# First four chunks of a retention and feed-forward kernel in another order, weight transfers to all partitions, other pacing

## The chip, the cores and the metric

The kernel runs on one core of one Trainium2 chip. The metric is the device time of one execution in microseconds (us). Five engines work side by side, each through its own queue in order: PE (matrix products, with PEld for its weight loads), DVE (the vector engine), ACT (the scalar engine), POOL (GpSimd) and SP, which here only issues transfers (DMAs).

## What is computed

```python
scores = scale * np.matmul(q, k.transpose(0, 1, 3, 2))     # 8 batches, 8 heads, 576 tokens, head width 64
ret = scores * Dmat                                        # gamma_h ** (t - s) for s <= t, else 0
attn_out = np.matmul(ret, v)
x = attn_out.transpose(0, 2, 1, 3).reshape(B * S, H * D)   # 4608 tokens x 512
h = np.maximum(x @ w_in, 0.0)                              # w_in 512 x 2048
return h * h @ w_out                                       # w_out 2048 x 512
```

`w_in` and `w_out` arrive as 64-bit floats. The kernel rounds them to 32 bits itself.

## The kernel before

**Retention in chunks.** Each batch's 576 tokens are cut in chunks of 128, 128, 128, 128 and 64 (`N_CH` = 40 in all), each of two halves of 64 tokens. For a chunk `load` brings k, q and v to tiles `k_ld`, `q_ld`, `v_ld` (one transfer each, on SP), and for the first five also a slice of the decay table `dq`. Then come

- `turn` (T below): 16 transposes of k and q on PE into `t_ps` (L363), a copy of k to `kT` on ACT (L369), and a product with `dq` to `qT` on DVE (L371);
- `scores` (S): products of `kT` and `qT` into `sc_ps` (L384), the mask on DVE into `ret` (L387), and the scaling of `v_ld` on POOL (L389). `t_ps` and `sc_ps` are one buffer, so that `turn` of the next chunk waits until DVE has read the scores;
- `retain_a` (X): the second half's own products into `x_ps` (L401), and the growth of the state in `u_ps` (L407), which ACT copies to `u_sb` (L413);
- `retain_b` (U): products of the state `u_sb` with `qT` into `x_ps` (L441);
- `retain_c` (X): the first half's own products and the second growth, and ACT's copy of the finished `x_ps` to the block of x (L462). `x_ps` is one buffer, so that the next `retain_a` waits for that copy.

**Feed-forward in blocks.** Nine blocks of 512 tokens. Block 0 is done by 16 plain steps `first_in` (each 4 products of 512 columns, L523; ACT's relu L528 and DVE's square L531 follow). Blocks 1 to 8 use a scheme with 7 products for 8 (`PRODUCTS`): 28 steps `ffn_in` each (L557), for which DVE first makes four sums of x (`sum_x`, L485 to L488), and sums of the results (L499 to L502) that SP writes to `g_dram` (L503). The second product with `w_out` (L736) runs behind all of this, from 640 us on.

**Conversion of the weights.** `w_in` comes in 16 pieces of 512 KB (`fetch_w`, before in two transfers of 64 partitions each, L184) into six raw buffers. Each piece takes five steps (`round_parts`): `one` (DVE L204, ACT L206), `two` (DVE L210, ACT L211), `three`, `four`, `five` (DVE L214, L217, L220). `convert(n)` emits the next n of these steps. A piece must be through before its `first_in`.

**What sets the order.** The program is written out by hand: per chunk `i` the main loop (L639) emits retain_a, retain_b, scores, turn and retain_c, with `convert` and `ffn` between them. `ffn` emits as many feed-forward steps as the pacing number `owed` allows, which grows with the chunk's tokens. Engines take what is emitted in that order, so that a step that waits holds all that is behind it on its engine. The steps of a block join the list `steps` when all its tokens are through.

## Time and profile before

| | us |
|---|---|
| median of 3 executions | 1045.21 (1044.27 to 1048.78) |
| the profiled execution | 1044.61 |
| its span, first to last instruction | 1042.8 |
| PE busy in it | 987.2 (95%) |
| DVE busy | 754.7 (72%) |
| ACT busy | 184.0 (18%) |
| POOL busy | 80.2 (8%) |

In the profile's rows a line reads: start or count, duration, engine, line of the kernel, operation, tile written, tiles read, shape, and in square brackets how long the engine was idle before and who ended that. One matrix product on 32-bit numbers is two records. PEclk is the granted clock of PE as a share of full speed.

### The profile page before, as it was taken

The numbers are of one execution on the slowest core, as the hardware profiler recorded it, in microseconds if no ns is written. First come the engines' busy times: TensorE is split into PE (matmuls) and PEld (weight loads), VectorE is DVE, ScalarE is ACT, GpSimd is POOL, SyncE is SP. The second block draws the span as 40 slices with busy tenths as digits, with TensorE's granted clock in tenths as the row PEclk, the third lists the DMA queues.
The fourth block names the chain that finished last, engine by engine and source line by source line (L and its number), as shares of the span: only waits on it lengthen the run. The fifth ranks groups of instructions, "written<-read, shape, count | busy, mean of one in ns | idle before, by whom it ended". The sixth has DMA issues, their size and how long they took to land.

```text
span 1042.8 us, 23785 instructions
## 1 busy us (share of the span) xinstructions
PE 987.2 (95%) x10376; PEld 868.3 (83%) x10376; DVE 754.7 (72%) x1398; ACT 184.0 (18%) x421; POOL 80.2 (8%) x82
## 2 busy tenths in 40 slices
PE   3699898999999999999999999999999999999998
PEld 2555457888887888878788788999999999999998
DVE  2567659766788888887796668677676777766775
ACT  2444322111221222222221110000000000000000
POOL 1111102001111101101011010000000000000000
PEclk9999899999999999999999999999999999999999
DMA  9998365645579778768746897853736536465351
GB/s 203 200 202 204 116 173 182 176 136 170 173 206 277 214 187 295 225 176 296 183 157 245 325 402 276 339 205 121 266 144 236 203 122 249 154 245 193 132 202 41
DMA packets 177927, 215.06 MB, mean 206 GB/s; under 512 B 116128, under 2 KB 126368, under 8 KB 168864
## 3 DMA queue, kind: packets, MB, share of 16 engines
q1 hardware_dynamic: 177824, 213.56, 65.2%
q8 instruction: 81, 1.33, 0.5%
q14 instruction: 22, 0.18, 0.1%
HBM read 125.19 MB, written 88.34 MB: 205 GB/s over the span
## 4 chain that ended last, share of the span: by engine, by line
PE 87%; DVE 7%; DMA 2%; ACT 2%; issue 1%; SPq 1%; ACTq 0%; DVEq 0%
PE o_b L736 16%; PE h_b L557 16%; PE o_c L736 10%; PE o_a L736 10%; PE h_c L557 10%; PE h_a L557 10%; PE h_ps L523 5%; PE x_ps L401 3%; PE t_ps L363 2%; PE x_ps L441 2%; PE sc_ps L384 2%; DMA a<-g_dram 1%; PE u_ps L407 1%; DVE room L564 1%; DVE ret L387 1%
## 5 line engine op out<-in xcount | busy, mean ns | idle before, releaser
L557 PE MATMUL h_b<-room,w 128*128 128x256 f32 x736 | 178.7, 386 | 7.5 <-DVE room L486 4.9
L557 PEld LDWEIGHTS h_b<-room,w 128*128 128x128 f32 x736 | 137.8, 191 | 28.5 <-issue 5.8
L736 PE MATMUL o_b<-w,room 128*128 128x128 f32 x1168 | 144.5, 275 | 1.3 <-DVE room L708 1.3
L736 PEld LDWEIGHTS o_b<-w,room 128*128 128x128 f32 x1168 | 137.2, 192 | 1.5 <-DVE room L708 1.4
L736 PE MATMUL o_c<-w,room 128*128 128x128 f32 x1008 | 123.0, 275 | 0.0
L736 PEld LDWEIGHTS o_c<-w,room 128*128 128x128 f32 x1008 | 117.7, 192 | 0.0
L557 PE MATMUL h_c<-room,w 128*128 128x256 f32 x480 | 115.6, 384 | 0.7 <-DVE room L571 0.7
L557 PE MATMUL h_a<-room,w 128*128 128x256 f32 x448 | 108.3, 385 | 0.0
L557 PEld LDWEIGHTS h_c<-room,w 128*128 128x128 f32 x480 | 89.6, 190 | 13.6 <-DVE room L571 1.1
L557 PEld LDWEIGHTS h_a<-room,w 128*128 128x128 f32 x448 | 84.2, 191 | 12.4 <-issue 0.5
L736 PE MATMUL o_a<-w,a 128*128 128x128 f32 x688 | 85.9, 275 | 1.3 <-DMA a<-g_dram 1.3
L736 PEld LDWEIGHTS o_a<-w,a 128*128 128x128 f32 x688 | 81.3, 192 | 1.5 <-issue 1.5
L564 DVE SCALAR_TENSOR_TENSOR room<-room 128x512 f32<-128x512 f32 x96 | 69.9, 728 | 3.3
L574 POOL TENSOR_TENSOR room<-room 128x512 f32<-128x512 f32 x32 | 34.4, 1075 | 460.4 <-ACT room L573 448.2
L401 PE MATMUL x_ps<-ret,v_ld 64*64 64x64 f32 x1152 | 54.9, 239 | 11.9 <-ACT room L462 9.1
L401 PEld LDWEIGHTS x_ps<-ret,v_ld 64*64 64x64 f32 x1152 | 44.7, 147 | 23.9 <-issue 20.6
L747 ACT COPY r<-o_a 128x128 f32<-128x128 f32 x54 | 14.4, 266 | 277.9 <-PE o_a L736 237.2
L523 PE MATMUL h_ps<-room,w 128*128 128x512 f32 x128 | 62.2, 631 | 0.0
L576 DVE TENSOR_TENSOR room<-h_b,room 128x512 f32<-128x512 f32 x32 | 22.1, 690 | 43.8 <-PE h_b L557 43.8
L389 POOL TENSOR_TENSOR v_ld<-v_ld,dv 128x512 f32<-128x512 f32 (+1 forms) x40 | 45.5, 1139 | 96.0 <-DMA v_ld<-in_v_dram 89.7
L387 DVE TENSOR_TENSOR ret<-sc_ps,msk 128x512 f32<-128x512 f32 (+1 forms) x40 | 27.4, 684 | 29.3 <-PE sc_ps L384 29.3
L407 PE MATMUL u_ps<-v_ld,k_ld 64*64 64x64 f32 x1024 | 47.6, 238 | 0.0
(92 smaller groups left out, 1330.0 us busy)
## 6 DMA issues: line engine op xcount, KB each, us to landing
g_dram<-room SPq DMA_DIRECT2D x36, 1792.0 KB, 7.3
a<-g_dram SPq DMA_DIRECT2D x43, 1024.0 KB, 6.1
room<-g_dram SPq DMA_DIRECT2D x20, 1024.0 KB, 6.2
w<-w_dram SPq DMA_DIRECT2D x7, 1792.0 KB, 10.9
out_dram<-room SPq DMA_DIRECT2D x18, 512.0 KB, 3.2
k_ld<-in_k_dram SPq DMA_DIRECT2D x32, 256.0 KB, 5.4
q_ld<-in_q_dram SPq DMA_DIRECT2D x32, 256.0 KB, 6.1
v_ld<-in_v_dram SPq DMA_DIRECT2D x32, 256.0 KB, 6.5
```

Source lines behind the costliest of these rows:

```text
L363: nc.tensor.transpose(p[:, h, j, hp, :], loaded[i][j][rows(h), 2 * hp:2 * hp + 2, :], ident[rows(h), rows(h)])
L384: nc.tensor.matmul(sc[rows(h), e, hp, :], lhsT=kT[rows(e), hp, t], rhs=qT[rows(e), hp, t], start=True, stop=True, skip_group_check=True)
L387: nc.vector.tensor_tensor(r[:cs], sc[:cs], msk[:cs].to_broadcast([cs, 2, HP, CH]), op=ALU.mult)
L389: nc.gpsimd.tensor_tensor(vs[:cs], vs[:cs], dv[:cs, :, ci:ci + 1].to_broadcast([cs, H, D]), op=ALU.mult)
L401: own.append(lambda g=g, e=e, b=b, head=head: nc.tensor.matmul(x_at(g, e, b, h), lhsT=s["vs"][rows(h), head, :], rhs=s["ret"][rows(h), e, ...
L407: grow.append(lambda hp=hp, e=e, head=head: nc.tensor.matmul(u_ps[0][rows(e), hp, :], lhsT=loaded[i][1][rows(1 - h), head, :], rhs=s["vs"] ...
L523: nc.tensor.matmul(p.rearrange("p h t -> p (h t)"), lhsT=w[:, c, :], rhs=xT[0][:, c, :], start=(c == 0), stop=(c == N_DM - 1))
L557: nc.tensor.matmul(p[:, mm, :], lhsT=w[:, c, :], rhs=xs[n][right][:, c, :], start=(j in OPENS and mm == 0 and c == 0), stop=(j in CLOSES a ...
L564: nc.vector.scalar_tensor_tensor(t, t, 0.0, t, op0=ALU.max, op1=ALU.mult)
L574: nc.gpsimd.tensor_tensor(g["A11"], g["A11"], g["A11"], op=ALU.mult)
L576: nc.vector.tensor_tensor(g["A22"], p, p15, op=ALU.add)
L736: nc.tensor.matmul(p, lhsT=s["lefts"][left][:, m, :], rhs=w_out[j][:, m, WO_SLOT[right], :], start=(i in OPENS and m == 0), stop=(i in CLO ...
```

## The change

- **First four chunks.** Chunks 0 to 3 (`N_EARLY`) run in a loop of their own, with no feed-forward step between: per turn of the loop retain_a, retain_b, retain_c of the chunk before, then scores and turn. Weight conversion begins at the second turn, and SP brings the first piece behind chunk 1's data instead of chunk 0's. `retain_c` of these chunks has a two-column copy on ACT ahead of its products (before, the last two chunks alone had it), so that these products wait for ACT.
- **w_in and the heads.** A piece of `w_in` is now one transfer to 128 partitions, in the weights' plain order. So that x comes out in that order, heads 4 and 5, and 6 and 7, change places in k and q while they are loaded: k and q are loaded in three transfers each (four heads, then two of two heads) instead of one, and the decay table is turned to match.
- **Pacing.** `first_in` steps run over 768 tokens instead of 1024, with four convert steps ahead of each instead of three; blocks 1 to 3 are spread over the next 1280 tokens; from there 28 steps for each 512 tokens, as before.
- **x in two parts.** In `retain_c` the state's copy now comes ahead of the copy of x; feed-forward steps that must come before x's buffer is written again are emitted between the two parts of a chunk that lies across two blocks; and a block's steps join the list right behind the copy.

```diff
         got = {}
         for name, src, pool in (("k", k, ld4), ("q", q, ld3), ("v", v, ld4)):
             t = got[name] = pool.tile([128, H, D], F32, tag=name, name=f"{name}_ld")
-            nc.sync.dma_start(t[:cs], src[b, :, c0:c0 + cs, :].rearrange("h s d -> s h d"))
+            at = src[b, :, c0:c0 + cs, :].rearrange("h s d -> s h d")
+            if name == "v":
+                nc.sync.dma_start(t[:cs], at)
+            else:
+                nc.sync.dma_start(t[:cs, 0:H // 2, :], at[:, 0:H // 2, :])
+                for e in range(2):
+                    nc.sync.dma_start(t[:cs, H // 2 + e::2, :], at[:, H // 2 + 1 - e::2, :])
             if i < NCH and name == "q":
                 nc.sync.dma_start(dq[:, :, c0:c0 + cs], decay_q[:, :, c0:c0 + cs])
         if i == 0:
...
         wi, m, e = pieces[j]
         f = (m + e * N_M) * 128
         if wi == 0:
-            return moe_w_in.rearrange("(b c d) f -> b d c f", b=2, c=N_DM)[:, :, :, f:f + 128]
+            return moe_w_in.rearrange("(c p) f -> p c f", p=128)[:, :, f:f + 128]
         return moe_w_out[f:f + 128, :].rearrange("p (c f) -> p c f", c=N_DM)
     def piece_dst(j):
...
-    def bring(t, j):
-        src = piece_src(j)
-        for b in range(2 if pieces[j][0] == 0 else 1):
-            if pieces[j][0] == 0:
-                nc.sync.dma_start(t[64 * b:64 * b + 64], src[b])
-            else:
-                nc.sync.dma_start(t, src)
     def fetch_w(j):
         if j < len(pieces) and wide:
-            bring(raw_of(j).bitcast(I64).rearrange("p (c f) -> p c f", c=N_DM), j)
+            nc.sync.dma_start(raw_of(j).bitcast(I64).rearrange("p (c f) -> p c f", c=N_DM), piece_src(j))
...
     nc.gpsimd.memset(exp_bias, -896.0 * 2.0 ** 23)
     for i in range(3):
         load(i)
-        fetch_raw(1)
+        fetch_raw(min(i, 1))
     ident = only.tile([128, 128], F32, name="ident")
     make_identity(nc, ident)
...
-    HEADS = [(g, e, b, 4 * b + 2 * g + e) for g in range(H // 4) for e in range(2) for b in range(2)]
+    HEADS = [(hp, e, e if hp < HP // 2 else 1 - e) for hp in range(HP) for e in range(2)]
...
-    def x_at(g, e, b, h):
-        return xp[0][rows(b), e, 0:256].rearrange("p (g t) -> p g t", g=2)[:, g, CH * h:CH * h + CH]
+    def x_at(hp, b, h):
+        return xp[0][rows(b), hp // 2, 0:256].rearrange("p (g t) -> p g t", g=2)[:, hp % 2, CH * h:CH * h + CH]
-        for g, e, b, head in HEADS:
-            own.append(lambda g=g, e=e, b=b, head=head: nc.tensor.matmul(
-                x_at(g, e, b, h), lhsT=s["vs"][rows(h), head, :], rhs=s["ret"][rows(h), e, 2 * b + g, :],
-                start=clears(b, e), stop=False, skip_group_check=True))
-        for hp in range(HP):
-            for e in range(2):
-                head = 2 * hp + e
-                grow.append(lambda hp=hp, e=e, head=head: nc.tensor.matmul(
-                    u_ps[0][rows(e), hp, :], lhsT=loaded[i][1][rows(1 - h), head, :], rhs=s["vs"][rows(1 - h), head, :],
-                    start=(ci == 0 and h == 1 and hp == 0), stop=(hp == HP - 1), skip_group_check=True))
+        for hp, e, b in HEADS:
+            own.append(lambda hp=hp, e=e, b=b: nc.tensor.matmul(
+                x_at(hp, b, h), lhsT=s["vs"][rows(h), 2 * hp + b, :], rhs=s["ret"][rows(h), e, hp, :],
+                start=clears(b, hp // 2), stop=False, skip_group_check=True))
+            grow.append(lambda hp=hp, e=e, b=b: nc.tensor.matmul(
+                u_ps[0][rows(e), hp, :], lhsT=loaded[i][1][rows(1 - h), 2 * hp + e, :], rhs=s["vs"][rows(1 - h), 2 * hp + b, :],
+                start=(ci == 0 and h == 1 and hp == 0), stop=(hp == HP - 1), skip_group_check=True))
...
             if 2 * ci + h == 0:
                 continue
             u = u_sb[(2 * ci + h) % 3]
-            for g in range(2):
-                for b in range(2):
-                    for e in range(2):
-                        nc.tensor.matmul(x_at(g, e, b, h), lhsT=u[rows(e), 2 * b + g, :],
-                                         rhs=s["qT"][rows(e), 2 * b + g, CH * h:CH * h + CH],
-                                         start=clears(b, e), stop=False, skip_group_check=True)
+            for hp, e, b in HEADS[0:2] + HEADS[4:6] + HEADS[2:4] + HEADS[6:8]:
+                nc.tensor.matmul(x_at(hp, b, h), lhsT=u[rows(e), hp, :], rhs=s["qT"][rows(e), hp, CH * h:CH * h + CH],
+                                 start=clears(b, hp // 2), stop=False, skip_group_check=True)
     def retain_c(i):
         b_, ci, c0, cs = chunks[i]
         own, grow = within(i, 0)
         more = ci + 1 < NCH
-        if i >= N_CH - 2:
-            nc.scalar.copy(u_sb[(2 * ci + (cs // CH)) % 3][:, 0:2, 0:1], xp[0][:, :, 0:1])
+        if i < N_EARLY or i >= N_CH - 2:
+            nc.scalar.copy(u_sb[(2 * ci + (cs // CH)) % 3][:, 0:2, 0:1], xp[0][:, :, cs - CH:cs - CH + 1])
         for j in range(0, len(own), 2):
             for f in own[j:j + 2] + (grow[j:j + 2] if more else []):
                 f()
+        if more:
+            grown(i, 1)
         tok = b_ * S + c0
         at = tok
-        p = xp[0][:, :, 0:256].rearrange("p e (g t) -> p e g t", g=2)
+        p = xp[0][:, :, 0:256].rearrange("p a (g t) -> p a g t", g=2)
         while at < tok + cs:
             n = at // TOK
+            while steps and steps[0][0] <= (n - 2 if n > 4 else n - 3):
+                step()
+                owed[0] -= 1
             end = min(tok + cs, (n + 1) * TOK)
-            nc.scalar.copy(xT[n][:, :, at - n * TOK:end - n * TOK].rearrange("p (g e) t -> p e g t", e=2),
+            nc.scalar.copy(xT[n][:, :, at - n * TOK:end - n * TOK].rearrange("p (a g) t -> p a g t", a=2),
                            p[:, :, :, at - tok:end - tok])
             at = end
-        if more:
-            grown(i, 1)
+            if n_next[0] < N_BLK and (n_next[0] + 1) * TOK <= at:
+                steps.extend(block_steps(n_next[0]))
+                n_next[0] += 1
         st[i] = loaded[i] = None
...
-            if 1 not in sums_x:
-                sums_x[1] = sum_x(1)
-                sums_w[0] = sum_w_in(0)
-            sums_x[1].pop(0)()
-            sums_w[0].pop(0)()
+            sums_w.setdefault(0, sum_w_in(0)).pop(0)()
+            if n_next[0] > 1:
+                if 1 not in sums_x:
+                    sums_x[1] = sum_x(1)
+                sums_x[1].pop(0)()
...
     n_next = [0]
+    R_0 = TOK * 3 // 2
+    LAG = 7
     def ffn(i):
         b, ci, c0, cs = chunks[max(0, min(i, N_CH - 1))]
-        n = (b * S + c0) // TOK
-        owed[0] += cs / 3 / TOK * {0: 0, 1: N_W1 / 2, 2: N_W1 / 2, 3: 2 * N_MP * NP}.get(n, N_MP * NP)
+        tok = b * S + c0
+        if tok < TOK + R_0:
+            rate = (N_W1 - 2) / R_0 if tok >= TOK else 0
+        elif tok < 5 * TOK:
+            rate = (3 * N_MP * NP - LAG) / (4 * TOK - TOK - R_0 + TOK)
+        else:
+            rate = N_MP * NP / TOK
+        owed[0] += cs / 3 * rate
         while steps and owed[0] >= 1:
             owed[0] -= 1
             if steps[0][0] == 0:
-                convert(3)
-            elif steps[0][0] == 3 and n_late:
-                owed[0] -= n_late.pop()
+                convert(4)
             step()
-    n_late = [5]
     turn(0)
     for i in range(N_CH + 1):
-        if i >= 1:
+        if i <= N_EARLY:
+            if i >= 1:
+                retain_a(i - 1)
+                retain_b(i - 1)
+                convert(2 if i >= 2 else 0)
+                retain_c(i - 1)
+            scores(i)
+            convert(1 if i >= 2 else 0)
+            if i == N_EARLY:
+                step()
+            turn(i + 1)
+            convert((0, 2, 2, 2, 3)[i])
+            if i == N_EARLY:
+                step()
+        else:
             retain_a(i - 1)
-        convert(2 if i < 6 else 1)
-        ffn(i - 1)
-        if i >= 1:
+            convert(1)
+            ffn(i - 1)
             retain_b(i - 1)
-        if i < N_CH:
-            scores(i)
-        convert(2 if i < 6 else 1)
-        ffn(i - 1)
-        if i + 1 < N_CH:
-            turn(i + 1)
-        if i >= 1:
-            b, ci, c0, cs = chunks[i - 1]
-            n = (b * S + c0 + cs - 1) // TOK
-            while steps and steps[0][0] <= (n - 2 if n > 4 else n - 3):
-                step()
+            if i < N_CH:
+                scores(i)
+            convert(1)
+            ffn(i - 1)
+            if i + 1 < N_CH:
+                turn(i + 1)
             retain_c(i - 1)
-        convert(1)
-        ffn(i - 1)
-        if i >= 1:
-            while n_next[0] < N_BLK and (n_next[0] + 1) * TOK <= b * S + c0 + cs:
-                steps += block_steps(n_next[0])
-                n_next[0] += 1
+            convert(1)
+            ffn(i - 1)
         if i + 3 < N_CH:
             load(i + 3)
-        if i < 6:
-            fetch_raw(1)
+        if i < N_EARLY:
+            fetch_raw(1 if i < 2 else 2)
     assert n_next[0] == N_BLK
     first.close()
...
-    gq = np.repeat(gt.reshape(H // 2, 2, 1, S), D, axis=2).reshape(H // 2, 2 * D, S).transpose(1, 0, 2)
+    pairs = gt.reshape(H // 2, 2, 1, S).copy()
+    pairs[H // 4:] = pairs[H // 4:, ::-1]
+    gq = np.repeat(pairs, D, axis=2).reshape(H // 2, 2 * D, S).transpose(1, 0, 2)
```

How the instructions of three places move (in the changed kernel the lines have other numbers: L364, L370 and L372 are T, L385 and L388 are S, L402 and L405 are X, L411 is the copy to `u_sb`, L437 U, L447 the two-column copy, L463 the copy of x, L202 to L218 the conversion, L487 to L490 the sums of x, L235 to L238 sums of `w_out`, L566 to L585 what a step `ffn_in` does on DVE; `w_89` to `w_95` are the weight tiles and raw buffers).

DVE at the start of the program, before:

```order
L371 TENSOR_TENSOR qT<-t_ps,dq 128x2x4x64
L204 TENSOR_SCALAR w_93<-w_93 128x512
L210 TENSOR_SCALAR w_89<-w_93 128x512
L387 TENSOR_TENSOR ret<-sc_ps,msk 128x512
L204 TENSOR_SCALAR w_94<-w_93 128x512
L210 TENSOR_SCALAR w_89<-w_93 128x512
L371 TENSOR_TENSOR qT<-t_ps,dq 128x2x4x64
```

and in the changed kernel:

```order
L372 TENSOR_TENSOR qT<-t_ps,dq 128x2x4x64
L388 TENSOR_TENSOR ret<-sc_ps,msk 128x512
L372 TENSOR_TENSOR qT<-t_ps,dq 128x2x4x64
L388 TENSOR_TENSOR ret<-sc_ps,msk 128x512
L372 TENSOR_TENSOR qT<-t_ps,dq 128x2x4x64
L202 TENSOR_SCALAR w_93<-w_93 128x512
L208 TENSOR_SCALAR w_89<-w_93 128x512
L202 TENSOR_SCALAR w_94<-w_93 128x512
```

The first two conversion steps (L204, L210) stood ahead of chunk 0's mask; they now stand behind the `qT` of chunk 2.

ACT from the `kT` of chunk 2, before:

```order
L369 COPY kT<-t_ps 128x2x4x64
L462 COPY room<-x_ps 128x2x2x128
L413 COPY u_sb_142<-u_ps 128x256
L413 COPY u_sb_140<-u_ps 128x256
L206 ACTIVATE w_94<-w_94,exp_bias 128x512
L211 ACTIVATE w_94<-w_94 128x512
```

and in the changed kernel:

```order
L370 COPY kT<-t_ps 128x2x4x64
L204 ACTIVATE w_93<-w_93,exp_bias 128x512
L209 ACTIVATE w_93<-w_93 128x512
L411 COPY u_sb_148<-u_ps 128x256
L204 ACTIVATE w_94<-w_94,exp_bias 128x512
L209 ACTIVATE w_93<-w_93 128x512
L447 COPY u_sb_149<-x_ps 128x2
L411 COPY u_sb_149<-u_ps 128x256
L463 COPY room<-x_ps 128x4x128
```

Before, the copy of x and both copies to `u_sb` came first and the conversion steps behind them. Now two conversion steps (L204, L209) stand ahead of the copy to `u_sb`, and two more ahead of the two-column copy.

DVE where one block of x follows another (the first step of a block, between the result sums of the block before), before:

```order
L499 TENSOR_TENSOR room<-room 128x512
L238 TENSOR_TENSOR w_95<-w_95 128x3x128
L485 TENSOR_TENSOR room<-room 128x512
L486 TENSOR_TENSOR room<-room 128x512
L487 TENSOR_TENSOR room<-room 128x2x256
L488 TENSOR_TENSOR room<-room 128x512
L500 TENSOR_TENSOR room<-room 128x512
```

and in the changed kernel, where they begin ahead of the result sums (L501 to L504 were L499 to L502):

```order
L487 TENSOR_TENSOR room<-room 128x512
L578 TENSOR_TENSOR room<-h_b,room 128x512
L566 SCALAR_TENSOR_TENSOR room<-room 128x512
L488 TENSOR_TENSOR room<-room 128x512
L235 TENSOR_TENSOR w_95<-w_95 128x3x128
L582 TENSOR_TENSOR room<-h_c,room 128x512
L566 SCALAR_TENSOR_TENSOR room<-room 128x512
L489 TENSOR_TENSOR room<-room 128x2x256
L236 TENSOR_TENSOR w_95<-w_95 128x3x128
L585 TENSOR_TENSOR room<-h_b,room 128x512
L566 SCALAR_TENSOR_TENSOR room<-room 128x512
L501 TENSOR_TENSOR room<-room 128x512
```

The four sums of x stood in one run of four; now three of them stand one by one between other steps, and the fourth follows three rows behind these.

4 lines of the change are left out of this document (3 added, 1 removed).

## The prediction

> **What bounds the kernel now.** I read three views in this order: the busy times in stretches, the chain of waits, and then PE's own waits. The first, cut at the kernel's stages (length, busy time of PE, PEld, DVE, ACT and POOL with counts, granted clock, DMA share, GB/s):
>
> ```profile
> 0.00:28.20 28.20, 8.59 (x192) 7.22 (x192) 7.41 (x14) 7.48 (x13) 4.48 (x13) 1.00 1.07 207
> 28.20:55.70 27.50, 20.24 (x489) 17.84 (x489) 16.76 (x29) 10.65 (x22) 4.71 (x4) 1.00 1.08 197
> 55.70:106.00 50.30, 47.21 (x658) 25.50 (x656) 37.28 (x63) 22.56 (x43) 7.13 (x6) 1.00 0.98 204
> 106.00:118.00 12.00, 8.67 (x88) 4.98 (x91) 8.60 (x12) 2.87 (x7) 2.02 (x2) 0.72 0.25 73
> 118.00:151.40 33.40, 31.11 (x458) 17.30 (x450) 18.07 (x29) 8.65 (x19) 0.00 (x0) 1.00 0.60 171
> 151.40:200.00 48.60, 45.32 (x380) 37.55 (x379) 41.20 (x62) 9.11 (x17) 6.40 (x5) 0.96 0.60 182
> 200.00:600.00 400.00, 390.77 (x4419) 328.05 (x4418) 313.99 (x517) 85.72 (x172) 51.31 (x49) 1.00 0.70 216
> 600.00:1042.80 442.80, 435.27 (x3717) 429.90 (x3715) 311.40 (x676) 37.02 (x132) 4.15 (x4) 1.00 0.55 207
> ```
>
> PE is the bound nearly everywhere, and its work is the same after the change (as many products of the same shapes). So the sum is made of lost PE time alone: idle time, and work at a low clock. PE idles 26.9 us up to 55.7 (28.2 - 8.59 + 27.5 - 20.24), 8.7 us in block 0 (55.7 to 151.4), 3.3 us up to 200, 9.2 us up to 600, and 7.5 us behind that, which the change doesn't touch.
>
> The first stage in the chain of waits (start, us, what):
>
> ```profile
> 12.27 5.75 DMA w<-in_moe_w_in_dram
> ...
> 30.03 1.14 PE x_ps L441 x32
> 31.16 0.90 PE sc_ps L384 x32
> 32.06 0.02 issue
> 32.08 0.70 DVE ret L387
> 32.78 0.04 issue
> 32.83 1.12 PE t_ps L363 x15
> ...
> 35.04 0.59 ACT room L462
> ...
> 37.18 0.38 ACT u_sb L413
> ```
>
> Two things bound it. Up to 18 us the chain goes over a weight transfer: DVE stands at a conversion step, and what retention needs is queued behind it on DVE. From 28 us on no transfer is on the chain; it is a relay between PE, DVE and ACT, one round per chunk. The first kind in PE's timeline, where the mask of chunk 0 came behind the first conversion steps:
>
> ```profile
> 12.61 0.69 PE L363 MATMUL t_ps<-ident,k_ld 64*128 64x64 f32 x8 [4.18 <-DVE ret L387]
> ```
>
> **The clock.** PE's timeline at block 0's first step, and around the one long wait in block 0:
>
> ```profile
> 55.65 4.87 PE L523 MATMUL h_ps<-room,w 128*128 128x512 f32 x8
> ...
> 105.04 0.65 PE L384 MATMUL sc_ps<-qT,kT 64*64 64x64 f32 x32
> 108.77 0.46 PE L363 MATMUL t_ps<-ident,k_ld 64*128 64x64 f32 x8 [3.08 <-DVE ret L387]
> ...
> 112.25 5.58 PE L523 MATMUL h_ps<-room,w 128*128 128x512 f32 x8
> ...
> 118.61 3.70 PE L523 MATMUL h_ps<-room,w 128*128 128x512 f32 x8
> ```
>
> After 3.08 us of idling the same block-0 step took 5.58 us instead of 3.70. And the scores of one chunk, 0.65 us here, took 0.90 us at 31.16: the first stage runs at the low clock too, although its rows say 1.00. The Trainium skill ("TensorE: Matmul & The Clock Gate", "What's actually happening") says that PE starts at half its clock and is let go only after about 3.4 us of sustained work. The trace agrees at 108.77, and it contradicts the clock column of the first two stretches.
>
> **A, the first stage.** Removed: the conversion steps on DVE ahead of chunk 0's and 1's masks, and 512 KB of weights ahead of chunk 1's data. Added: four more issues on SP per chunk, and in retain_c a copy on ACT that PE waits for. I add up the new relay from the durations above, at the low clock. By bytes (1.5 MB at 207 GB/s, and some 3 us ahead of the first byte) chunk 1's k and q land at about 11; by SP's queue later (rows of its timeline, and of the table of issues, whose last number is the us to landing):
>
> ```profile
> 48.38 0.58 SPq L132 DMA_DIRECT2D q_ld<-in_q_dram  x1
> ```
>
> ```profile
> k_ld<-in_k_dram SPq DMA_DIRECT2D x32, 256.0 KB, 5.4
> ```
>
> and, of ACT's timeline, two conversion steps:
>
> ```profile
> 33.14 0.72 ACT L206 ACTIVATE w<-w,exp_bias 128x512 uint32<-128x512 uint32 x1 [3.17 <-DVE w L204]
> 33.77 0.65 ACT L211 ACTIVATE w<-w 128x512 f32<-128x512 uint32 x1
> ```
>
> 15 issues of 0.58 us from 0.8 on and 4 to 5.4 us of landing give 13.5 to 15 for the transposes (T) of chunk 1 (now 12.6); I take 13.5, since the queue is not full so early. A round is then T 1.1, retain_a 1.3 (between the end of the copy of x at 35.63 and the u_sb copy at 37.18), that copy with its handing over 0.5, retain_b 1.1, the new copy 0.4 (as the u_sb copy), retain_c 1.1 (from T's end at 33.95 to the copy of x at 35.04), scores 0.9, mask 0.8: 7.2 us, and 6.7 for chunk 0, whose retain_b is half. The new copy waits for PE's retain_b; behind it on ACT are the state's copy and the copy of x, which come later than it anyway, and PE's retain_c waits for it. ACT makes it longer: the two conversion steps (L206, L211: from 33.14 to 34.42, 1.3 us for the pair) stand ahead of the u_sb copy once, and ahead of the two-column copy in each of three rounds, with up to 0.5 us of DVE before them. I take 8.9, 8.6 and, for the last one with its small T, 6.8 us up to block 0's first step: 13.5 + 6.7 + 8.9 + 8.6 + 6.8 = 44.5, against 55.7 now. The weights it converts land in time (piece 2 by bytes at 30, used at 32). What was done before 55.7 and isn't before 44.5 (T of chunks 5 and 6, scores 5, retention of the short chunk 4) costs 2.8 us of PE at the full clock later. **A = 55.7 - 44.5 - 2.8 = 8.4 us**; bounds 13 (no delay on ACT) and 2 (a round more on SP and ACT).
>
> **B, block 0.** PE's waits in 55.7 to 151.4 (total, times, longest):
>
> ```profile
> PE x_ps L401 <- ACT w L462: 2.9, 4, 0.8
> PE x_ps L401 <- ACT room L462: 2.3, 3, 0.8
> ```
>
> with the 3.08 us above: 8.7 us idle, and about 4.1 us at the low clock (1.2 at its first step, 1.9 at 112.25, 1 in the small products there). In the changed order seven of the eight rounds have a block-0 step between scores and T, so that the mask is covered by 3.7 us; three pairs of retain_c and retain_a stay without a step between (2.2 us), two state copies lie open (1.0), one mask (0.8), and the first step's cold start stays (1.2). Against it DVE gets fuller:
>
> ```profile
> 55.70:106.00 50.30, 34.42 (x72) 13.48 (x72) 1.00 0.98 204
> ```
>
> This row is L523 alone: nine steps. So DVE worked 37.28 / 9 = 4.1 us per step, and PE 47.21 / 9 = 5.2. With 2.33 steps per chunk instead of 2, PE has 3.7 + 12.8 / 4.5 / 2.33 = 4.9 us per step and DVE some 4.2: 86% instead of 79%. I put one more stall of 6 us (as at 108.77, with its cold products) at even odds: 3 us. **B = 12.8 - 8.2 = 4.6, taken as 4**; bounds -8 (two or three such stalls) and 8.
>
> **C, block 1.** Waits in 151.4 to 200:
>
> ```profile
> PE h_b L557 <- DVE room L576: 2.5, 1, 2.5
> ```
>
> Here DVE is busy 41.2 of 48.6 us, and the clock's 0.96 costs 1.9 us more. The 28 steps of block 1 now lie beside 3.6 chunks instead of 2, so that DVE's sums get more PE time. **C = 3.5 of 5.2**; bounds 0 and 5.
>
> **D, blocks 1 to 8.** Waits in 200 to 600:
>
> ```profile
> PE h_b L557 <- DVE room L486: 4.9, 3, 1.8
> PE x_ps L401 <- ACT room L462: 2.9, 4, 0.8
> PE t_ps L363 <- DVE ret L387: 1.4, 2, 1.1
> ```
>
> The first goes where the sums of x no longer stand in one run (three times 1.6); the second where a step now stands between retain_c and retain_a everywhere; two open state copies of 0.5 come in. **D = 6 of 9.2**; bounds 2 and 8.
>
> **At nothing:** the other order of heads (as many products, of the same shapes, in the same four quarters of the array: the row at 30.03 stays as it is; bounds -1 and 1, 4% of the time that L441 takes in all); one weight transfer for two (same bytes; bounds 0 and 2, in A). The 160 added issues (93 us of SP) are hidden because loads run three chunks ahead. POOL's row shows by how much, where it is tight:
>
> ```profile
> 102.15 1.34 POOL L389 TENSOR_TENSOR v_ld<-v_ld,dv 128x512 f32<-128x512 f32 x1 [13.41 <-DMA v_ld<-in_v_dram]
> ```
>
> That v is first read behind the T at 108.77, over 5 us later; four more issues ahead of it take 2.3.
>
> The sum: 1044.6 (the profiled execution: span 1042.8 and 1.8 around it; the median of the three runs is 0.6 higher) - 8.4 - 4 - 3.5 - 6 = **1022.7 us**.
>
> **The rivals.**
> - *DVE bounds block 0* (0.16). For it: 86%, and a wait there throws PE to the low clock. Against it: a step of 3.7 us covers nearly every mask. B becomes -4: 1031.
> - *Small transfers hold the first stage* (0.12). For it: the queue is full there (DMA share 1.07). If the 20 added issues of five chunks all count (11.6 us, less 2 that overlap), block 0 starts at 54 and A is -1: 1032. The Trainium skill ("DMA: Bandwidth & Descriptors", "Measured") has 64 KB transfers at 138 GB/s and 1 MB at 341, and calls transfers under 64 KB descriptor-dominated. By that the four 64 KB parts of a chunk would cost some 0.6 us more, an estimate of 3 us over five chunks and a sum of 1026; no run here shows a 64 KB transfer.
> - *The first chunks run at the full clock* (0.10), since nothing but PE's own rounds is left. Against it: 20.24 of 27.5 us busy wasn't enough before. 5.8 us of PE per round would shrink by 0.4 of it, three times: 1016.
> - *Slower: the loads come late* (0.06). If SP, behind weight transfers that wait for DVE's last conversion step, brings a chunk's v more than 5 us later against PE, PE idles at every chunk of block 0: six times 2.3 us and some 3 us of low clock, 30 us: 1053.
> - *The start is given back* (0.04): the pieces of w_in set block 0's end, A and B are nothing, half of C and D stays: 1040.
>
> **How the numbers follow.** My forecast (1016 to 1029) has 0.52. The range 1010 to 1036 takes in the first three rivals and the bounds of A to D as far as they fall together, and leaves out the last two and the tails. A measurement of this kernel tells some 0.5% (5 us) from no change: faster by more than that 0.86, within it 0.08, slower 0.06.
>
> **What would show it.** Right: the first L523 step (now L525) near 44 us; no wait over 2 us for the mask in block 0; no wait for L486 (now L488); PE idle from 200 to 600 us near 3. Wrong: block 0's start past 50 us with PE waiting for transfers; DVE over 90% busy in block 0 with PE waiting for the mask or for conversion; POOL's waits for v followed by waits of PE.

## The result, and the profile after

| | before | changed |
|---|---|---|
| median, us | 1045.53 (1044.27 to 1048.78) | 1019.22 (1017.67 to 1020.46) |
| ratio | 1 | 0.9743, 95% interval 0.9715 to 0.9771 |
| profiled execution, us | 1044.61 | 1018.01 |
| its span, us | 1042.8 | 1016.3 |
| PE busy, us | 987.2 | 978.9 |
| PE idle, us | 55.6 | 37.4 |

The kernel became 2.6% faster, and the forecast of 1022.7 us was 3.5 us too high. The span lost 26.5 us: 18.2 of idle time on PE, and 8.3 of busy time. The products are the same, so the busy time that went is put down to work at the low clock.

The busy times in stretches of the changed kernel, cut at its own stages (length, busy time of PE, PEld, DVE, ACT, POOL with counts, granted clock, DMA share, GB/s):

```profile
0.00:43.50 43.50, 24.55 (x584) 20.64 (x584) 13.22 (x24) 14.17 (x30) 7.87 (x16) 1.00 0.87 206
43.50:130.20 86.70, 82.09 (x1015) 44.42 (x1016) 71.00 (x119) 36.53 (x68) 8.52 (x7) 1.00 0.74 204
130.20:200.00 69.80, 69.80 (x836) 58.46 (x836) 56.69 (x90) 15.33 (x30) 11.17 (x10) 1.00 0.66 195
200.00:600.00 400.00, 394.16 (x4354) 331.32 (x4353) 315.26 (x517) 83.95 (x169) 51.94 (x48) 1.00 0.71 231
600.00:1016.30 416.30, 408.30 (x3592) 406.09 (x3590) 294.09 (x651) 34.60 (x128) 1.04 (x1) 1.00 0.53 198
```

The idle time of a stage is its length less PE's busy time. The first stage went from 26.9 to 19.0 us, block 0 from 8.7 to 4.6, what follows up to 200 us from 3.3 to nothing, 200 to 600 from 9.2 to 5.8, and the rest from 7.5 to 8.0. None of these stretches shows 0.72 or 0.96 of the clock, as two did before.

PE's timeline of the changed kernel, at chunk 1's transposes, at the four longest waits behind them and at block 0's start (start, us, engine, line, operation, and in brackets the idle time before and who ended it):

```profile
10.29 0.69 PE L364 MATMUL t_ps<-ident,k_ld 64*128 64x64 f32 x8 [0.88 <-DVE ret L388]
...
17.67 0.92 PE L364 MATMUL t_ps<-ident,k_ld 64*128 64x64 f32 x8 [1.55 <-DMA k_ld<-in_k_dram]
...
22.79 1.13 PE L437 MATMUL x_ps<-qT,u_sb 64*64 64x64 f32 x32 [2.30 <-ACT u_sb L411]
...
25.21 0.37 PE L402 MATMUL x_ps<-ret,v_ld 64*64 64x64 f32 x2 [1.29 <-ACT u_sb L447]
...
28.02 0.69 PE L364 MATMUL t_ps<-ident,k_ld 64*128 64x64 f32 x8 [0.82 <-DVE ret L388]
...
33.54 0.37 PE L402 MATMUL x_ps<-ret,v_ld 64*64 64x64 f32 x2 [1.71 <-ACT u_sb L447]
...
36.34 0.69 PE L364 MATMUL t_ps<-ident,k_ld 64*128 64x64 f32 x4 [0.81 <-DVE ret L388]
...
43.54 4.23 PE L525 MATMUL h_ps<-room,w 128*128 128x512 f32 x8 [0.20 <-ACT room L463]
```

Block 0 begins at 43.54 us. T of chunks 1 to 4 stands at 10.29, 17.67, 28.02 and 36.34: the rounds take 7.4, 10.4, 8.3 and 7.2 us. Two waits make the second one long: the 2.30 us at 22.79 for the copy to `u_sb` (L411), ahead of which ACT has the first pair of conversion steps, and 1.29 us for the two-column copy. The chain of waits shows the second of them (start, us, what):

```profile
17.80 5.57 DMA w<-in_moe_w_in_dram
23.39 0.44 DVE w L202
23.85 0.72 ACT w L204
24.57 0.54 ACT w L209
25.21 0.37 PE x_ps L402 x2
```

The second weight piece lands at 23.4. Its conversion steps on DVE and ACT stand ahead of the two-column copy (L447), which PE waits for. Up to there the chain goes over SP's issues (to 10.25 us) and two weight transfers; the relay takes over behind it.

### The profile page after: what moved, and what is told of

It reads as the page before. It is cut to its first block, busy times and chain, and to the rows that moved or that the text cites. A ratio compares the mean times of both kernels' runs of the same rounds, so it can differ in the third digit from the quotient of the medians.

```text
span 1016.3 us, 23980 instructions
## 1 busy us (share of the span) xinstructions
PE 978.9 (96%) x10376; PEld 860.9 (85%) x10376; DVE 750.3 (74%) x1398; ACT 184.6 (18%) x425; POOL 80.5 (8%) x82
## 4 chain that ended last, share of the span: by engine, by line
PE 89%; DVE 5%; DMA 3%; ACT 1%; SPq 1%; issue 1%; DVEq 0%; ACTq 0%
PE o_b L748 16%; PE h_b L559 16%; PE o_c L748 11%; PE o_a L748 11%; PE h_a L559 10%; PE h_c L559 10%; PE h_ps L525 6%; PE x_ps L402 4%; PE t_ps L364 2%; PE x_ps L437 2%; PE sc_ps L385 2%; DMA a<-g_dram 1%; DMA w<-in_moe_w_in_dram 1%; DVE room L566 1%; PE u_ps L405 1%
## 5 line engine op out<-in xcount | busy, mean ns | idle before, releaser
L566 DVE SCALAR_TENSOR_TENSOR room<-room 128x512 f32<-128x512 f32 x96 | 71.0, 739 | 3.3
L402 PEld LDWEIGHTS x_ps<-ret,v_ld 64*64 64x64 f32 x1152 | 42.4, 143 | 23.4 <-issue 13.9
L402 PE MATMUL x_ps<-ret,v_ld 64*64 64x64 f32 x1152 | 52.6, 234 | 9.2 <-ACT u_sb L447 5.3
L525 PE MATMUL h_ps<-room,w 128*128 128x512 f32 x128 | 59.7, 610 | 0.2 <-ACT room L463 0.2
L372 DVE TENSOR_TENSOR qT<-t_ps,dq 128x512 f32<-128x512 f32 (+1 forms) x40 | 25.4, 634 | 36.1 <-ACT kT L370 25.8
L755 DVE TENSOR_TENSOR small<-o_b,small 128x128 f32<-128x128 f32 x63 | 18.4, 291 | 40.2 <-PE o_b L748 40.2
```

Source lines behind the costliest of these rows:

```text
L372: nc.vector.tensor_tensor(to, p[:, :n_h, j, :, :], dq[:, :, c0:c0 + cs].rearrange("p d (h t) -> p h d t", h=n_h), op=ALU.mult)
L402: own.append(lambda hp=hp, e=e, b=b: nc.tensor.matmul(x_at(hp, b, h), lhsT=s["vs"][rows(h), 2 * hp + b, :], rhs=s["ret"][rows(h), e, hp, : ...
L525: nc.tensor.matmul(p.rearrange("p h t -> p (h t)"), lhsT=w[:, c, :], rhs=xT[0][:, c, :], start=(c == 0), stop=(c == N_DM - 1))
L566: nc.vector.scalar_tensor_tensor(t, t, 0.0, t, op0=ALU.max, op1=ALU.mult)
```

## The experiments

Each kernel is the changed one with one edit. The last column is the difference from the changed kernel, from the two ratios, in us of the time before; the changed kernel's own interval is 2.9 us to each side, so that differences under 4 us are read from the traces beside it.

| kernel | median, us | ratio to before, 95% interval | against the changed, us |
|---|---|---|---|
| e3_order_back | 1041.33 | 0.9958 (0.9945 to 0.9970) | +22.5 |
| e3b_order_back_in_step | 1027.24 | 0.9813 (0.9794 to 0.9832) | +7.3 |
| e2_pacing_back | 1040.88 | 0.9947 (0.9934 to 0.9961) | +21.3 |
| e2b_rates_back | 1038.07 | 0.9917 (0.9894 to 0.9939) | +18.2 |
| e10_block0_slow | 1032.73 | 0.9876 (0.9855 to 0.9897) | +13.9 |
| e1_heads_back | 1021.39 | 0.9769 (0.9754 to 0.9783) | +2.7 |
| e4_x_back | 1022.35 | 0.9775 (0.9763 to 0.9788) | +3.3 |
| e6_lag3 | 1020.82 | 0.9765 (0.9752 to 0.9778) | +2.3 |
| e6_lag5 | 1016.51 | 0.9713 (0.9698 to 0.9727) | -3.1 |
| e5_conv_behind | 1017.79 | 0.9723 (0.9706 to 0.9740) | -2.1 |
| e8_busy | 1014.28 | 0.9695 (0.9678 to 0.9712) | -5.0 |
| e9_busy_lag5 | 1009.71 | 0.9660 (0.9647 to 0.9672) | -8.7 |

### The order of the first four chunks

e3: chunks 0 to 3 in the old order (conversion from the start, scores and T ahead of retain_c, no two-column copy), all else as changed.

```diff
-        fetch_raw(min(i, 1))
+        fetch_raw(1)
-        if i < N_EARLY or i >= N_CH - 2:
+        if i >= N_CH - 2:
         if i <= N_EARLY:
+            convert(2)
             if i >= 1:
                 retain_a(i - 1)
                 retain_b(i - 1)
-                convert(2 if i >= 2 else 0)
-                retain_c(i - 1)
             scores(i)
-            convert(1 if i >= 2 else 0)
-            if i == N_EARLY:
-                step()
+            convert(2)
             turn(i + 1)
-            convert((0, 2, 2, 2, 3)[i])
-            if i == N_EARLY:
-                step()
+            if i >= 1:
+                retain_c(i - 1)
+            convert(1)
```

> The changed kernel with chunks 0 to 3 in the old order (scores and turn between retain_b and retain_c, conversion from the first chunk on, the first weight piece behind chunk 0, no two-column copy there). My theory (term A is the order and the weights on the chain): block 0 begins at 53 to 57 us and the time is 1027 to 1031. Rival, that most of the 12 us come from elsewhere (pacing, or block 0's steps joining the list earlier): block 0 begins before 50, 1019 to 1024.

Measured: 1041.33 us, some 10 more than the theory allowed. Block 0 begins at 55.31 us, as in the kernel before and as the theory had it, but 22 us are more than the start. The busy times from 200 to 600 us, PE's waits for the mask there (total, times, longest), and PE's timeline behind the longest of them:

```profile
200.00:600.00 400.00, 387.03 (x4337) 325.27 (x4336) 309.28 (x506) 84.62 (x170) 53.32 (x48) 0.98 0.67 210
```

```profile
PE t_ps L364 <- DVE ret L388: 7.9, 5, 3.5
```

```profile
394.17 3.37 PE L559 MATMUL h_a<-room,w 128*128 128x256 f32 x8
```

The old order leaves out the two steps that the new one emits itself, the pacing stays two steps behind, and twice (behind the scores at 387.9 and at 525.9 us) no step stands between scores and T. The first time the mask is open for 3.49 us, and the next step takes 3.37 us instead of 1.99. From 200 to 600 us PE idles 13.0 us instead of 5.8, at 0.98 of the clock. So the same loop with `owed` begun at 2:

```diff
+    owed[0] = 2.0
```

> As e3_order_back, but with two block-0 steps emitted ahead of time, so that from chunk 5 on the order of steps is that of the changed kernel; in e3 it lagged by two, and two masks late in the program had no step beside them. My theory (the order of the first four chunks is worth term A alone, and e3's rest was those two open masks, 3 to 5 us each with the low clock behind them): block 0 begins near 53 to 55, no wait over 2 us for the mask behind 250 us, 1027 to 1032. Rival, that the old order costs 20 us by itself: 1038 to 1042.

Measured: 1027.24 us. From 200 to 600 us PE's longest wait for the mask is 0.8 us again. Block 0's first two steps, emitted earlier than in e3 and earlier than the theory had them, stand in PE's timeline at

```profile
50.49 9.63 PE L525 MATMUL h_ps<-room,w 128*128 128x512 f32 x16 [1.01 <-ACT room L463]
```

which is 6.95 us later than in the changed kernel, and the time is 7.3 us longer. That is what the order is worth where the pacing is in step with it, as closely as the two intervals (2.0 and 2.9 us to each side) tell.

### The pacing

e2: the old rates and three conversion steps ahead of each `first_in`; e2b: the old rates alone, with four.

```diff
-        tok = b * S + c0
-        if tok < TOK + R_0:
-            rate = (N_W1 - 2) / R_0 if tok >= TOK else 0
...
-        owed[0] += cs / 3 * rate
+        n = (b * S + c0) // TOK
+        owed[0] += cs / 3 / TOK * {0: 0, 1: N_W1 / 2, 2: N_W1 / 2, 3: 2 * N_MP * NP}.get(n, N_MP * NP)
...
-                convert(4)
+                convert(3)
+            elif steps[0][0] == 3 and n_late:
+                owed[0] -= n_late.pop()
```

> The changed kernel with the old pacing number: 16 block-0 steps over 1024 tokens with three conversion steps each, blocks 1 and 2 within 512 tokens. My theory (terms B and C come from pacing): block 1 waits for DVE again (some 3 us and 2 us of low clock), and open masks come back in block 0: 1024 to 1029 us. Rival, that the pacing gives nothing and the other parts carry B and C: 1019 to 1021, no wait of PE for DVE between 130 and 220 us.

> As e2_pacing_back, but with four conversion steps ahead of a block-0 step, as in the changed kernel: only the rates at which steps are emitted are the old ones. My theory (the rates bring the open masks in block 0 and the sums of x in one run, and squeeze block 1): the three waits of PE for DVE's conversion (4.0 us in e2) go, the rest stays: 1033 to 1038, sums of x waited for five or six times. Rival, that e2's loss was conversion that came late: 1020 to 1026.

Measured: 1040.88 and 1038.07 us; the first is 12 us beyond its theory's range, the second at the edge of its own. In e2, with the new order and the old pacing, block 0 begins at 42.43 us, 13 us ahead of the kernel before, and only 5.5 us of that reach the end. PE's waits and two stretches of e2b:

```profile
PE t_ps L364 <- DVE ret L388: 9.0, 8, 1.9
PE h_b L559 <- DVE room L488: 8.5, 6, 1.8
```

```profile
43.50:130.20 86.70, 78.41 (x1114) 42.47 (x1110) 69.52 (x115) 36.33 (x69) 10.02 (x8) 1.00 0.71 194
...
200.00:600.00 400.00, 387.79 (x4359) 323.62 (x4358) 313.26 (x510) 85.04 (x171) 51.40 (x48) 1.00 0.68 222
```

The idle time is 8.3 us in block 0 instead of 4.6, 3.6 instead of nothing from there to 200 us, and 12.2 from 200 to 600 instead of 5.8. The sums of x stand in one run again for four blocks, and PE waits for them six times. Between e2 and e2b lies the number of conversion steps; the 3 us between them hardly exceed the intervals, but e2 alone has waits of PE for the conversion (4.0 us in three, for L218).

e10 parts the rates: the 14 steps of block 0 that the loop paces over 1024 tokens, blocks 1 to 3 evenly over the next 1024.

```diff
-        if tok < TOK + R_0:
-            rate = (N_W1 - 2) / R_0 if tok >= TOK else 0
+        if tok < 3 * TOK:
+            rate = (N_W1 - 2) / (2 * TOK) if tok >= TOK else 0
         elif tok < 5 * TOK:
-            rate = (3 * N_MP * NP - LAG) / (4 * TOK - TOK - R_0 + TOK)
+            rate = (3 * N_MP * NP - LAG) / (2 * TOK)
```

> Rates alone, split: block 0's steps go over 1024 tokens again, and blocks 1 to 3 follow over the next 1024 (38.5 steps for 512 tokens, evenly); order, conversion, heads, x and the lag of 7 stay as changed. Theory (most of what the new rates are worth lies in block 0, where a step stands between scores and T): four or five rounds of chunks 4 to 11 have no step there, each leaves the mask open (0.8 to 1.9 us, and as much again at the low clock), PE's idle time from 43 to 150 us rises from under 5 to 9 us or more, no wait for the sums of x (L488), and the time is 1027 to 1031. Rival (the rates are worth what they are because blocks 1 to 3 are evened out, and 1024 tokens for block 0 cost nothing by themselves): idle in block 0 stays under 6 us, the time is 1019 to 1022.

Measured: 1032.73 us, a little above what the theory gave. Stretches and PE's waits from 43.5 to 150 us:

```profile
43.50:130.20 86.70, 75.66 (x1040) 40.88 (x1038) 64.59 (x106) 34.04 (x64) 10.29 (x9) 0.92 0.64 173
130.20:176.00 45.80, 43.13 (x518) 32.04 (x519) 34.15 (x55) 12.44 (x24) 5.17 (x4) 1.00 0.67 195
```

```profile
PE t_ps L364 <- DVE ret L388: 6.9, 5, 3.3
```

The same waits in the same window of e2b, and then of the changed kernel:

```profile
PE t_ps L364 <- DVE ret L388: 2.7, 2, 1.9
...
PE t_ps L364 <- DVE ret L388: 0.8, 1, 0.8
```

The stretch that was block 0 now has 11.0 us of idle time and 0.92 of the clock. From 176 to 600 us PE idles 5.6 us, as in the changed kernel (5.8). So masks that stand open in block 0, with the low clock behind them, cost most of the 14 us. This is not block 0's share of the 18 us of the old rates, though. The edit spreads 14 steps over 1024 tokens where the old rate has 16: it leaves five masks behind block 0's start without a step between scores and T, the old rates (e2b) leave two, and the changed kernel one. What the old rates cost is read from e2b's own idle time: 3.7 us in block 0, 3.6 from there to 200 us, and 6.4 from 200 to 600, of the 17.0 us between the two spans.

### Heads, transfers and x in two parts

e1: k and q in one transfer each, w_in in two of 64 partitions, the old order of heads.

```diff
-                nc.sync.dma_start(t[:cs, 0:H // 2, :], at[:, 0:H // 2, :])
-                for e in range(2):
-                    nc.sync.dma_start(t[:cs, H // 2 + e::2, :], at[:, H // 2 + 1 - e::2, :])
+            nc.sync.dma_start(t[:cs], src[b, :, c0:c0 + cs, :].rearrange("h s d -> s h d"))
...
-            return moe_w_in.rearrange("(c p) f -> p c f", p=128)[:, :, f:f + 128]
+            return moe_w_in.rearrange("(b c d) f -> b d c f", b=2, c=N_DM)[:, :, :, f:f + 128]
```

> The changed kernel (1019.2 us, ratio 0.974 to before) with the heads, the decay table and the w_in transfers as before: k and q in one transfer each, w_in in two. My theory (edits at nothing, SP's issues hidden): 1019 within 2 us, block 0 begins between 42 and 44 us as in the changed kernel (43.5). Rival, that small transfers hold the first stage: block 0 begins 4 us earlier or more, near 39, and the time falls to 1015 or below. Rival, that one full-width weight transfer moves faster: block 0 begins later than 45.

Measured: 1021.39 us, just outside what the theory gave. Block 0's first step:

```profile
44.20 5.83 PE L531 MATMUL h_ps<-room,w 128*128 128x512 f32 x8 [0.19 <-ACT room L469]
```

T of chunk 5 stands 2.3 us later (50.0 against 47.7), but only 0.7 of that is block 0's start, and the rest its first step, 5.83 us instead of 4.23. Both vary as much without this edit: the kernels of e2, e2b, e10, e6_lag3 and e6_lag5 have the changed kernel's first stage word for word, and there block 0 begins between 42.43 and 44.15 us with a first step of 4.26 to 5.72. Here too the chain goes over SP's issues and a weight transfer, up to 24.0 us. The edit undoes the small transfers of k and q and the single transfer of w_in together, and the two were not parted; their net is 2.7 us in favour of the change, inside the changed kernel's interval. By the 64 KB and 1 MB figures of the Trainium skill ("DMA: Bandwidth & Descriptors", "Measured") going back to 256 KB should have gained an estimated 3 us; these runs do not show such a gain.

e4: the copy of x, the forced steps and the joining of a block as before.

```diff
     def retain_c(i):
-        if more:
-            grown(i, 1)
...
-            while steps and steps[0][0] <= (n - 2 if n > 4 else n - 3):
-                step()
-                owed[0] -= 1
...
-            if n_next[0] < N_BLK and (n_next[0] + 1) * TOK <= at:
-                steps.extend(block_steps(n_next[0]))
-                n_next[0] += 1
+        if more:
+            grown(i, 1)
```

> The changed kernel with the copy of x as before: the forced steps ahead of retain_c, the state's copy behind the copy of x, a block's steps joining the list behind the chunk's last steps. My theory (term D: the earlier joining lets the sums of x stand apart): PE waits for the sums again two or three times, 1.6 us each, and the time is 1022 to 1025. Rival, that the longer lag of the pacing alone does it: no such wait, 1018 to 1021.

Measured: 1022.35 us, the theory's time without the theory's waits: none for the sums of x comes back. Waits for the copy of x do (its line is L457 here; 1.1 us in one wait in the changed kernel):

```profile
PE x_ps L402 <- ACT room L457: 3.9, 5, 0.8
```

So x in two parts spares at most the waits for that copy (3.3 us by the ratios, not clear of noise), and it isn't what spreads the sums of x.

### The lag

Blocks 1 to 3 are paced so that they end `LAG` steps behind their tokens. e6_lag3 and e6_lag5 change this number alone (`-    LAG = 7`, `+    LAG = 3` and `+    LAG = 5`).

> Only the lag of blocks 1 to 3 behind their tokens is 3 steps instead of 7. Theory (it is this lag that lets the sums of x of the next block begin before the last one's steps are through, so that they stand apart): for two blocks the sums stand in one run again, PE waits for L488 there, 1.4 us each, and the time is 1020.5 to 1022.5; some of it comes back since fewer steps are forced ahead of x's copy. Rival (the sums stand apart because a block joins the list right behind its copy): no wait for L488, time as changed, 1018.5 to 1020.

> The changed kernel with a lag of 5 steps instead of 7 and nothing else. Theory (the 4.6 us between the two fastest kernels are the lag's own: fewer steps forced in one run ahead of x's copy, and no sums of x in one run yet): PE's idle time from 200 to 600 us falls from 5.8 to about 2.5, no wait for L488, 1014 to 1016. Rival (they come from the unread products as well, or from the clock of one profiled execution): 1018 to 1020, as changed.

Measured: 1020.82 us, as the theory gave, and 1016.51, half a us above it. PE's waits of lag 3:

```profile
PE h_b L559 <- DVE room L488: 3.4, 2, 2.0
```

and the stretch from 200 to 600 us of lag 5:

```profile
200.00:600.00 400.00, 397.58 (x4371) 334.71 (x4370) 317.07 (x523) 85.58 (x170) 51.16 (x48) 1.00 0.72 235
```

With 3 the wait for the sums of x is back for two blocks: it is the lag that spreads them. With 5 the sums stay apart and PE idles 2.4 us instead of 5.8. The second product begins 4.0 us earlier (609.56 against 613.57), of which 0.7 are there at block 0's start already; the median gains about 3, within the intervals. What went can be seen in the changed kernel's own PE timeline, behind a run of six steps forced ahead of a copy of x:

```profile
501.02 1.99 PE L559 MATMUL h_b<-room,w 128*128 128x256 f32 x8 [1.24 <-DVE room L578]
...
504.30 0.27 PE L402 MATMUL x_ps<-ret,v_ld 64*64 64x64 f32 x2 [1.28 <-issue]
```

### The first stage: conversion on ACT, and the clock

e5: in the early loop the two conversion steps come behind the products of retain_c.

```diff
-                convert(2 if i >= 2 else 0)
                 retain_c(i - 1)
+                convert(2 if i >= 2 else 0)
```

> The changed kernel with the two conversion steps of each early round behind retain_c instead of ahead of it, so that the two-column copy doesn't wait for them on ACT, nor for a weight piece. My theory (these steps stretch a round by 1.2 to 1.7 us, three times): the waits of PE for the two-column copy fall from 1.7 and 1.2 us to 0.5, block 0 begins between 39 and 41.5 us, 1015 to 1017. Rival, that the weights' arrival or the mask on DVE takes their place: block 0 begins at 43, 1018 to 1020.

Measured: 1017.79 us, a little above the theory's range. Waits, block 0's first step, and the scores of one chunk much later:

```profile
PE x_ps L402 <- ACT u_sb L447: 1.9, 5, 0.7
```

```profile
39.75 4.88 PE L525 MATMUL h_ps<-room,w 128*128 128x512 f32 x8 [0.20 <-ACT room L463]
...
503.10 1.10 PE L385 MATMUL sc_ps<-qT,kT 64*64 64x64 f32 x32
```

In the changed kernel this wait is 5.3 us, its longest 1.7. Block 0 begins 3.8 us earlier, at the low clock. The kernel leads by 3.0 us up to 487 us (T at 486.65 against 489.61) and by 1.4 at the second product's first step. Between them lie the two waits at a run of six forced steps that the changed kernel has too (at 501.02 and 504.30 there), but here the granted clock falls behind them (0.62 from 502 to 506 us against 1.00) and the scores take 1.10 us. The rest of the lead is lost at the low clock behind a wait for `a`. Nothing in the traces ties either to the edit; whether its 3 us reach the end in most executions stays open, since the intervals overlap.

e8: e5, and seven products of 128 columns on `ident` in each round, whose output is read by nothing.

```diff
+    def busy(n):
+        for _ in range(n):
+            nc.tensor.matmul(idle_ps[:, 0, 0:128], lhsT=ident, rhs=ident, start=True, stop=True, skip_group_check=True)
             if i >= 1:
                 retain_a(i - 1)
+                busy(2)
                 retain_b(i - 1)
-                convert(2 if i >= 2 else 0)
+                busy(2)
                 retain_c(i - 1)
+                convert(2 if i >= 2 else 0)
             scores(i)
+            busy(3 if i >= 1 else 0)
```

> As e5_conv_behind, with products that nobody reads (128 columns, into a free buffer) put where PE waits in the rounds of chunks 0 to 3: two behind retain_a, two behind retain_b, three behind the scores. Theory (activity lifts the clock; the first stage runs at the low one): from some 25 us on the scores of a chunk take 0.65 us instead of 0.90, block 0 begins at 35 to 38.5 us and its first step takes 3.7 us, 1011 to 1014. Rival, that the relay over ACT and DVE sets the round, or that the added products only fill it: scores stay at 0.90, block 0 begins at 39.5 or later, 1015 to 1019.

Measured: 1014.28 us, at the upper edge of the theory's range. PE's timeline, an added product (L650), the scores of chunk 3, block 0's first step and a later one:

```profile
30.73 0.71 PE L650 MATMUL idle_ps<-ident 128*128 128x128 f32 x4
31.89 0.65 PE L385 MATMUL sc_ps<-qT,kT 64*64 64x64 f32 x32
...
38.38 3.60 PE L525 MATMUL h_ps<-room,w 128*128 128x512 f32 x8
...
76.11 5.26 PE L525 MATMUL h_ps<-room,w 128*128 128x512 f32 x8
```

The scores take 0.65 us; in the changed kernel those of the first stage at 26.12 and 34.44 take 1.08 in the timeline. Block 0 begins 5.2 us earlier, with a step of 3.60 instead of 4.23 us. So the first stage comes to the full clock when PE gets more to do. Whether the share of busy time does it or the size of the added products (128 rows and columns instead of 64) was not parted. The Trainium skill ("TensorE: Matmul & The Clock Gate", "What's actually happening") says that about 3.4 us of sustained work release it. The trace agrees only for dense work: from 10 to 28 us in the changed kernel PE is busy 10.97 of 18 us and stays slow.

Little of this lead lasts in the profiled execution. At block 0's start e8 is 1.4 us ahead of e5, with a first step 1.3 us shorter. Behind a wait of 1.67 us for a copy of x at 75.39 the clock falls (0.73 from 74 to 78 us), a step takes 5.26 us, and at 486 us the lead over e5 is 0.5 us. The other 3 us between the two spans come behind 612 us, where e8 waits 1.4 us for `a` and keeps the clock, and e5 waits 2.9 and doesn't.

e9: e8 with a lag of 5.

> The fastest so far (conversion behind the products of retain_c, seven unread 128-column products in each round of the first stage) with a lag of 5 instead of 7. Theory (seven steps of lag are more than the sums need, and each step too many is forced in one run of six ahead of x's copy, where ACT and DVE then fall behind): 1013 to 1014, 0.5 to 1 us below lag 7. Rival (the sums need the whole lag): a wait for L488 of 1.4 us or two comes back, 1015 to 1017.

Measured: 1009.71 us, ratio 0.9660 (0.9647 to 0.9672): the fastest, beyond its theory's range, and faster than the changed kernel by more than both intervals. Its gain over e8, 3.7 us by the ratios, was forecast as 0.5 to 1, and is clear of both intervals too. PE's idle time from 200 to 600 us is 2.4 us here, as with lag 5 alone, instead of e8's 5.8; and e8's clock falls behind the run of six forced steps, as in e5 (0.57 from 502 to 506 us), while e9 has no such fall.

## Why the prediction held, and where its terms were off

| term | predicted, us | measured, us |
|---|---|---|
| A, first stage | 8.4 | 9.3 (55.65 - 43.54 - 2.8) |
| B, block 0 | 4 | about 9 (what the others leave of 26.5), some 7.6 by its own rows |
| C, block 1 | 3.5 | 5.2 (3.3 idle, 1.9 of low clock) |
| D, 200 to 600 us | 6 | 3.4 |
| behind it | 0 | -0.5 |

- **A** was right in size, and in its mechanism from 23.4 us on: a relay of PE, DVE and ACT with the conversion ahead of the two-column copy. Up to there the chain goes over SP's issues and weight transfers, which the prediction took to land in time. Two of its parts were off and nearly cancelled. SP's queue did not hold chunk 1's data (T at 10.3, not 13.5). Instead the weights came late: their first transfer on the chain begins at 10.30, behind SP's issues. The rounds took 33.3 us instead of 31, the second one above all, in which the copy to `u_sb` waits behind one pair of conversion steps and the two-column copy behind the next, whose weight piece lands at 23.4. The 2.8 us for work put off were not measured by themselves. e3b puts the order at 7.3 us. The prediction set scores of 0.90 us, from the chain, beside 0.65 from the timeline; the timeline has 1.08 for the first stage.
- **B** was the term that was mis-sized, and it lies past its upper bound of 8. Its own rows give 4.1 us of idle time and an estimated 3.5 of the low clock (4.1 before; now the first step's 4.23 instead of 3.70 us is left); the rest of the 9 isn't assigned. The prediction kept 3 us for one more long stall, because DVE would be fuller, and let 5.2 us of open masks, state copies and cold start stay. DVE did get full at its peak (18.87 of 20 us from 90 to 110 us; 71.0 of 86.7 in the whole block, below the forecast 86%), but PE idles 4.6 us in the whole block, its longest wait for a mask is 0.8, and the clock stays at 1.00. The steps between scores and T come from block 0's new rate, and not from the changed order that the prediction names: with the new order and the old rates (e2b) a mask at 104 us has no step beside it, as in the kernel before, and PE waits 1.92 us for it.
- **C** came whole, a little above its bound of 5, and e2b shows that it needs the rates: with the old ones 3.6 us are idle between 130 and 200 us.
- **D** had the sign right and the size wrong. The 4.9 us of waits for the sums of x went as predicted, and by the lag (e6_lag3), not by x in two parts (e4). "Near 3" for the idle time was not reached, since the lag of 7 brings runs of six forced steps that the prediction did not price; lag 5 gives 2.4.
- **At nothing**: the heads and the transfers. e1 gives 2.7 us in their favour, more than the 2 allowed, but within the intervals, and its trace shows 0.7 at block 0's start, less than that start varies by; the added issues are hidden, as predicted.
- **The rivals.** That DVE bounds block 0, that small transfers hold the first stage, that loads come late, and that the start is given back all fell for this kernel, the second as far as e1 can show it with both kinds of transfer undone at once. The last is what the order does without the pacing (e2). The first chunks at the full clock did not happen by themselves; e8 makes it happen, and 0.5 us of it against e5 is left at 486 us, where that rival's price was 6.7.
- **The parts don't add.** By the ratios the pacing without the order (e3) gains 4.4 us, the order without the pacing (e2) 5.5, both 26.9. With the old rates the early start is spent again on PE's waits in all stages behind it (e2b), and the new rate fits only if the first two steps stand where the order puts them (e3, e3b).
- **The closeness.** The sum came within 5 us because D, 2.6 too much, took back part of what A, B and C had too little.

## What to carry to other kernels

When a relay between engines is interleaved with dense steps, count the dense steps between each hand-over and its use: here a rate that left five masks in block 0 without a step instead of one cost 14 us, and a start 13 us earlier with the old pacing brought 5.5. Remove the longest open waits first, since they cost low clock as well. A few unread products can bring the clock up where the work is too thin for it, but here most of what they gained was lost again at the next long wait. Re-tune a pacing number (here the lag) after the structure has changed: it holds two costs against each other, and its best value moves.

## What was not expected of the hardware

- The granted clock reads 1.00 in the first stage although its products run slow: scores of 1.08 us there against 0.65. e3 has both readings over the same work: scores of 1.08 us under 1.00 and under 0.50.

```profile
28.00:34.00 6.00, 4.46 (x144) 3.90 (x144) 4.09 (x6) 1.52 (x4) 1.06 (x1) 1.00 0.77 177
40.00:55.00 15.00, 10.78 (x246) 9.52 (x248) 8.06 (x14) 5.95 (x12) 2.82 (x3) 0.50 0.80 203
```

```profile
30.67 1.08 PE L385 MATMUL sc_ps<-qT,kT 64*64 64x64 f32 x32
...
51.33 1.08 PE L385 MATMUL sc_ps<-qT,kT 64*64 64x64 f32 x32
```

- Seven added products in a round of some 7 us brought the full clock between 25.7 and 31.9 us (PE busy 14.66 of 18 us from 10 to 28); the changed kernel's own small products, busy 10.58 of 15.5 us from 28 to 43.5, did not.
- A wait of 2.5 to 2.9 us for `a` at the start of the second product stands in ten of these kernels. In eight the clock behind it reads 0.96 over some 40 us, which is an estimated 1.6 us of time; in the changed kernel and e2 it does not fall. The two rows show it for the changed kernel and for e5. So differences of a few us between single kernels can be this alone.

```profile
600.00:640.00 40.00, 36.95 (x268) 34.93 (x267) 30.25 (x59) 3.23 (x10) 1.04 (x1) 1.00 0.91 358
```

of the changed kernel, against

```profile
600.00:640.00 40.00, 36.89 (x260) 35.03 (x258) 28.89 (x56) 3.05 (x9) 1.04 (x1) 0.96 0.90 355
```

of e5. What decides between the two wasn't tried; the two waits near 500 us are another such pair (1.00 in the changed kernel, 0.62 in e5).
